# Weight conversion of a fused attention and two-MLP kernel: clamps moved to VectorE, rounding to ScalarE, cache writes to the sync queue, later loads spread, one more buffer set

## The chip, the cores and the metric

The kernel runs on one core of a Trainium2 chip. The metric is device microseconds of one execution, the median of several. A core has five engines that run side by side, each through its own list of instructions in a fixed order: TensorE (PE in the rows; PEld is its weight load), VectorE (DVE), ScalarE (ACT), GpSimd (POOL) and SyncE (SP, which here only issues DMAs). ACT issues some DMAs too (its rows are ACTq). An engine that waits for something holds up everything that stands behind it in its list.

## What is computed

The weights of both MLPs come as float64, everything else as float32. Shortened:

```python
def reference(q, k, v, phi, w_in, w_out, moe2...):
    a = softmax(phi, axis=sequence)                   # 4 batches x 8 heads, 576 tokens, 32 memories
    k_m, v_m = a^T @ k, a^T @ v                       # 32 x 64 each
    x = softmax(q @ k_m^T / 8) @ v_m                  # heads joined: 2304 x 512
    h = x @ w_in                                      # 512 -> 2048
    x = (h * sigmoid(1.702 * h)) @ w_out              # 2048 -> 512
    xn = x / sqrt(mean(x * x) + 1e-6) * rms_g
    g = xn @ w_gate                                   # 512 -> 1536
    return (g * sigmoid(g) * (xn @ w_val)) @ w_o2     # 1536 -> 512
```

## The kernel before

**Passes.** The four batches are two pairs (batches 0 and 1, batches 2 and 3). A batch has two units of four heads, so a pair has four units, named (batch, half). The first MLP goes over its hidden units in 8 groups of 256, once for each pair; `a_g1` makes a group's hidden values for a quarter of a pair's tokens, `a_g2` adds their product with `w_out` to the sum `x2`. The second MLP then goes over 6 groups (`b_g3`, `b_g4`) for all tokens. The RMS norm of a pair (`norm_1` to `norm_4`) lies between.

**Products.** Every float32 product is three passes on TensorE: a value is a high part (rounded to a shorter format) plus a low part (the rest). `copy` makes the high part and `sub_lo` the low part; both are helpers, so all their instructions have the lines L102 (copy on GpSimd), L106 (copy on another engine) and L109.

**Weights.** A group's weights are loaded as raw float64 halves of 128 x 512 (`w_load`, three raw buffers) and turned into float32 by bit operations (`w_conv`): absolute value on ACT (L152), clamp (L153), shift and mask (L157), sign (L161), low bits (L164) on DVE, then the high and low part. What the first pair's pass has worked out for the first MLP is written to a cache in device memory (L168), from which the second pair's pass loads it (L127). Of the 68 halves that are converted from float64, 32 belong to the first MLP and 36 to the second.

**Attention of a pair** runs ahead of its pass: `ld_phi` and `ld_src` load phi, k, v and q of a unit (144 KB twice, then 576 KB each), `att_k1` to `att_k5` make k_m and v_m, `att_q1` to `att_q4` the softmax. The second pair's four units are side work (`att_side`) that is issued between the first pair's groups, before time 300 us. A unit's k, v and q take one of six large buffers, which units, the transposed softmax and x2 share.

**Order.** The source issues steps by hand-written tables; a scheduler then sets the order of each engine's list, so an edit of one step can move others. PSUM and SBUF buffers come from pools that rotate. `gf`, the result of the gelu in `a_g1`, has three buffers of the tag "val", shared by both halves of a group.

**DMAs** take turns on eight semaphore lanes: a DMA on a lane waits in its engine's list until the DMA that had the lane before has landed, whichever engine issued it.

Of the kernel before, what the change touches and what calls it, by code (L numbers as in the profile page):

```python
# [18 lines left out]
def kernel(  # L19
# [14 lines left out]
    """Every float32 product is taken as three float32r passes: x = h + l exactly, h being x  # L34
    rounded to float32r, and x*y = h*h' + l*h' + h*l' in float32 accumulation.

    Attention: attn @ v_m @ w_in is taken as attn @ (v_m @ w_in), per batch and head. Two batches
    (a pair) share the array when v_m @ w_in is worked out. The MLPs run feature-major over blocks
    of their hidden units (256 wide), so each weight is loaded and split once per pass; the sums
    over blocks are kept in SBUF.  # L40

    Columns of a pair: batch, parity, chunk pair, p, for token 6 p + 2 (chunk pair) + parity.
    """
# [7 lines left out]
    P = 128  # L51
# [11 lines left out]
    MINW = 2.0**-15  # bits 0x38000000  # L63
    MAXW = 122872.0  # bits 0x47EFFC00
# [47 lines left out]
    # The first MLP's float32 weights, as they are worked out on the first pass over them.  # L112
# [29 lines left out]
    def w_conv(hf, clamp=G, to_h=G, to_l=G):  # L142
        """float64 to float32, on the bits: sign and top exponent bit, then the other exponent
        bits and the fraction 3 to the left. What is out of float32's range is clamped."""
# [3 lines left out]
        else:  # L148
# [4 lines left out]
            clamp.tensor_scalar(  # L153
# [13 lines left out]
            if hf[0] == "a":  # L167
                nc.scalar.dma_start(out=cached(hf), in_=t.bitcast(F32))  # L168
# [5 lines left out]
        copy(to_h, h[:, c], x)  # L174
        sub_lo(to_l, l[:, c], x, h[:, c])

# [1 line left out]
    # A unit is four heads of a batch. Where its k and v lay, q^T and the softmax of its scores follow.  # L178
    # The four 32-row blocks of an odd batch hold heads 2, 3, 0, 1.
# [245 lines left out]
        # An odd batch's heads 2, 3, 0, 1 lie in its blocks, so the rows' halves  # L425
        # are of different batches.
# [14 lines left out]
    gt, x2 = {}, {}  # L441

    def a_g1(pr, g, t):
# [4 lines left out]
        for fc in range(2):  # L448
# [10 lines left out]
            gf = tmp.tile([P, TB], F32, tag="val", name="gf")  # L459
# [194 lines left out]
    def do(step):  # L654
        step[0](*step[1:])
# [15 lines left out]
    # Side work of each pass, in the order of its issue.  # L671
    def att_side():
        for u in [(2, 0), (2, 1), (3, 0), (3, 1)]:
            yield ld_unit, u
# [6 lines left out]
            yield from att_q(u, G)  # L681
# [30 lines left out]
    # Batch 0 first: its share of the first MLP runs beside the rest of batch 1's attention.  # L712
    for s in (
# [11 lines left out]
        (att_k5, b0), (att_k5, b1), (w_load, w0[3]), (w_conv, w0[1], G, A), (vm_part, 0, 0, 0),  # L725
        (vm_part, 0, 0, 1), (att_q4, a0, 0), (att_q4, a1, 1), (att_q4, a0, 1), (w_conv, w0[2]),
        (att_q4, a1, 0), (narrow,), (att_q1, b1, 1), (w_conv, w0[3], G, A), (w_load, w1[0]),
        (att_q1, b0, 0), (w_load, w1[1]), (w_conv, w1[0], G, A), (att_q1, b1, 0), (att_q3, b1, 1),
# [88 lines left out]
```

## Time and profile before

| | |
|---|---|
| device time, median of 3 runs | 922.57 us (921.31 to 928.22) |
| the profiled execution: span from first to last instruction | 919.6 us |
| busy: PE, PEld, DVE, ACT, POOL | 866.3, 823.1, 556.7, 382.2, 496.5 us |
| instructions | 14798 |

The profiled execution is told by its span; its own time is not listed apart. The span leaves out what lies before the first and after the last instruction, and the median of the runs stands 3.0 us above it. Rows name an engine, a line of the source (L153), an operation and the tiles that it writes and reads; a time in square brackets or behind "idle before" is how long that engine had nothing to run, with what ended the wait.

### The profile page before, as it was taken

Reading aid. Unit: us, or ns where it says so; the run is one execution under the profiler, and the core shown is the slowest. Engines: PE = TensorE matmul, PEld = TensorE weight load, DVE = VectorE, ACT = ScalarE, POOL = GpSimd, SP = SyncE. Lnnn points to the kernel's source line nnn. Section 1 sums busy time; section 2 is a strip of 40 time slices with the busy share of each in tenths; the row PEclk is TensorE's granted clock in tenths of the full one; section 3 lists DMA queues with packets and bytes.
Section 4 is the critical chain, followed back from the end, with each engine's and each line's share of the span. In section 5 each row is a group of like instructions: output and inputs, shape, how many; then the busy total and the mean of one; then the engine's idle time right before and its main releaser. Section 6 shows DMA issues by size and latency. Waiting matters only on the chain.

```text
span 919.6 us, 14798 instructions
## 1 busy us (share of the span) xinstructions
PE 866.3 (94%) x5702; PEld 823.1 (90%) x5702; DVE 556.7 (61%) x997; ACT 382.2 (42%) x823; POOL 496.5 (54%) x450
## 2 busy tenths in 40 slices
PE   3887997997999999999998999999999999999997
PEld 2776997986999999999988999999999999999997
DVE  5699896788965456558778155366348328333333
ACT  2366773654667765554466342122122122111110
POOL 2377998897987695979994162064046018001000
PEclk9989998999999999999999999999999999999999
DMA  9974559433221120223313021012004001000123
GB/s 215 258 218 124 165 137 244 160 118 108 90 70 46 48 69 25 69 73 101 92 47 92 1 92 46 1 46 92 0 1 124 14 1 47 1 1 1 46 58 103
DMA packets 40534, 74.62 MB, mean 81 GB/s; under 512 B 3856, under 2 KB 16144, under 8 KB 40464
## 3 DMA queue, kind: packets, MB, share of 16 engines
q1 hardware_dynamic: 35856, 65.29, 26.2%
q10 hardware_dynamic: 4608, 8.39, 2.6%
q8 instruction: 45, 0.74, 0.3%
q14 instruction: 25, 0.20, 0.1%
HBM read 60.56 MB, written 13.11 MB: 80 GB/s over the span
## 4 chain that ended last, share of the span: by engine, by line
PE 72%; POOL 8%; DVE 7%; DMA 6%; issue 4%; SPq 2%; ACT 1%; ACTq 0%; POOLq 0%; DVEq 0%
PE pg L577 31%; PE pg L608 16%; PE pg L483 14%; PE pg L454 7%; POOL cv L153 2%; DMA stage<-in_k_dram 2%; DVE cv L161 2%; PE pvm L422 2%; DMA raw_a_out<-in_moe_w_out_dram 2%; POOL gr L109 2%; DVE cv L164 1%; DVE x L491 1%; DMA stage<-in_v_dram 1%; DVE cv L157 1%; DMA raw_a_in<-in_moe_w_in_dram 1%
## 5 line engine op out<-in xcount | busy, mean ns | idle before, releaser
L483 PE MATMUL pg<-gr,a_outh 128*128 128x288 f32 x1024 | 231.4, 301 | 11.7 <-DVE x L491 10.2
L483 PEld LDWEIGHTS pg<-gr,a_outh 128*128 128x128 f32 x1024 | 172.8, 190 | 16.4 <-DVE x L491 14.7
L483 PE MATMUL pg<-gr,a_outl 128*128 128x288 f32 x512 | 151.6, 297 | 0.0
L153 POOL TENSOR_SCALAR cv<-cv 128x512 f32<-128x512 f32 x67 | 137.1, 2051 | 22.8 <-ACT cv L152 20.8
L608 PE MATMUL pg<-b_o2h,pp 128*128 128x512 f32 x432 | 139.7, 391 | 0.0
L586 DVE TENSOR_TENSOR pf<-sg,pg 128x384 f32<-128x384 f32 x72 | 39.6, 552 | 158.2 <-PE pg L577 151.0
L109 POOL TENSOR_TENSOR gr<-gf,gr 128x288 fp32r<-128x288 f32 x128 | 115.9, 920 | 34.8 <-ACT gr L462 30.1
L491 DVE TENSOR_TENSOR x<-x,pg 128x288 f32<-128x288 f32 x224 | 95.9, 446 | 61.8 <-PE pg L483 60.7
L102 POOL TENSOR_SCALAR b_o2h<-cv 128x512 fp32r<-128x512 f32 x12 | 8.4, 716 | 223.6 <-PE pg L577 223.4
L584 ACT ACTIVATE sg<-pg 128x384 f32<-128x384 f32 x72 | 35.4, 492 | 159.1 <-PE pg L577 159.0
L483 PEld LDWEIGHTS pg<-gr,a_outl 128*128 128x128 f32 x512 | 97.1, 190 | 0.0
L608 PEld LDWEIGHTS pg<-b_o2h,pp 128*128 128x128 f32 x432 | 81.1, 188 | 16.1
L588 ACT CAST pp<-pf 128x384 fp32r<-128x384 f32 x72 | 37.0, 513 | 126.9 <-DVE pf L586 126.6
L608 PE MATMUL pg<-b_o2l,pp 128*128 128x512 f32 x216 | 84.8, 393 | 0.0
L616 DVE TENSOR_TENSOR oacc<-oacc,pg 128x512 f32<-128x512 f32 x90 | 61.1, 683 | 24.1 <-PE pg L608 24.1
L460 ACT ACTIVATE gf<-pg 128x288 f32<-128x288 f32 x128 | 51.6, 410 | 53.4 <-POOL gr L109 25.2
L109 DVE TENSOR_TENSOR pp<-pf,pp 128x384 fp32r<-128x384 f32 x72 | 46.3, 643 | 34.9 <-ACT pp L588 34.9
L462 ACT CAST gr<-gf 128x288 fp32r<-128x288 f32 x128 | 53.5, 432 | 28.8 <-PE pg L483 25.3
L577 PE MATMUL pg<-xnh,b_gateh 128*128 128x384 f32 x288 | 62.6, 337 | 0.0
L577 PE MATMUL pg<-xnh,b_vall 128*128 128x384 f32 x288 | 62.3, 337 | 0.0
L577 PE MATMUL pg<-xnh,b_gatel 128*128 128x384 f32 x288 | 62.3, 336 | 0.0
L157 DVE TENSOR_SCALAR cv<-cv 128x512 uint32<-128x512 uint32 x68 | 52.0, 765 | 17.0 <-POOL cv L153 16.9
(183 smaller groups left out, 1849.4 us busy)
## 6 DMA issues: line engine op xcount, KB each, us to landing
raw_a_in<-in_moe_w_in_dram SPq DMA_DIRECT2D x16, 512.0 KB, 4.2
raw_a_out<-in_moe_w_out_dram SPq DMA_DIRECT2D x16, 512.0 KB, 4.3
cache<-cv ACTq DMA_DIRECT2D x32, 256.0 KB, 3.8
raw_b_gate<-in_moe_w_gate_dram SPq DMA_DIRECT2D x12, 512.0 KB, 3.7
raw_b_val<-in_moe_w_val_dram SPq DMA_DIRECT2D x12, 512.0 KB, 3.8
raw_b_o<-in_moe_w_out_dram SPq DMA_DIRECT2D x12, 512.0 KB, 3.6
stage<-in_k_dram SPq DMA_DIRECT2D x8, 576.0 KB, 12.1
stage<-in_v_dram SPq DMA_DIRECT2D x8, 576.0 KB, 11.6
```

What stands on the lines that cost most here:

```text
L109: eng.tensor_tensor(out=lo, in0=full, in1=hi.bitcast(F32), op=ALU.subtract)
L153: clamp.tensor_scalar(out=t.bitcast(F32), in0=t.bitcast(F32), scalar1=MINW, scalar2=MAXW, op0=ALU.max, op1=ALU.min,)
L157: nc.vector.tensor_scalar(out=t, in0=t, scalar1=3, scalar2=0x3FFFFFFF, op0=ALU.logical_shift_left, op1=ALU.bitwise_and,)
L454: nc.tensor.matmul(ps[:, :HALF], lhsT=a[:, b, c, f], rhs=at[:, y, c, n], start=(i == 0), stop=(i == 5),)
L460: nc.scalar.activation(out=gf[:, :HALF], in_=ps[:, :HALF], func=AF.Gelu_apprx_sigmoid)
L462: nc.scalar.copy(out=gr[:, 0, :HALF], in_=gf[:, :HALF])
L483: nc.tensor.matmul(ps[:, :HALF], lhsT=wo[a][:, fc, es], rhs=gr[fc][:, y, :HALF], start=(i == 0), stop=(i == 5),)
L491: nc.vector.tensor_tensor(out=acc[:, e, n], in0=acc[:, e, n], in1=ps[:, :HALF], op=ALU.add)
L577: nc.tensor.matmul(ps[:, :TB], lhsT=w[a][:, e, f], rhs=xs[y][:, e, n], start=(i == 0), stop=(i == 3 * NE - 1),)
L586: nc.vector.tensor_tensor(out=pf, in0=sg, in1=pss[1][:, :TB], op=ALU.mult)
L608: nc.tensor.matmul(ps, lhsT=pp[fc][:, a, ks], rhs=w[y][:, fc], start=(i == 0), stop=(i == 5))
L616: nc.vector.tensor_tensor(out=o, in0=o, in1=ps, op=ALU.add)
```

## The change

It does five things. The clamp of every converted half runs on VectorE (before: 67 of 68 on GpSimd). The high part of a freshly converted half is rounded on ScalarE (before: 62 of 68 on GpSimd, 6 on ScalarE by hand); halves that come from the cache stay on GpSimd. Cache writes are issued by SyncE instead of ScalarE. The loads of the second pair's units 2 to 4 are issued one by one beside the query steps of the unit before, instead of at the head of their own unit. The gelu's second half takes a buffer of the tag "sg" (three buffers that only the second MLP used). In the start-up table the arguments that had put single steps elsewhere are dropped, and one half's low part goes to VectorE as before.

```diff
-    def w_conv(hf, clamp=G, to_h=G, to_l=G):
+    def w_conv(hf, to_h=None, to_l=G):
...
-            clamp.tensor_scalar(
+            nc.vector.tensor_scalar(
                 out=t.bitcast(F32), in0=t.bitcast(F32), scalar1=MINW, scalar2=MAXW,
...
             if hf[0] == "a":
-                nc.scalar.dma_start(out=cached(hf), in_=t.bitcast(F32))
+                nc.sync.dma_start(out=cached(hf), in_=t.bitcast(F32))
...
-        copy(to_h, h[:, c], x)
+        copy(to_h or (G if hf[:2] == ("a", 1) else A), h[:, c], x)
         sub_lo(to_l, l[:, c], x, h[:, c])
...
-            gf = tmp.tile([P, TB], F32, tag="val", name="gf")
+            gf = tmp.tile([P, TB], F32, tag=("val", "sg")[fc], name="gf")
...
     def att_side():
-        for u in [(2, 0), (2, 1), (3, 0), (3, 1)]:
-            yield ld_unit, u
+        us = [(2, 0), (2, 1), (3, 0), (3, 1)]
+        yield ld_unit, us[0]
+        for u, nxt in zip(us, us[1:] + [None]):
             yield att_k1, u
...
-            yield from att_q(u, G)
+            for i, step in enumerate(att_q(u, G)):
+                if nxt and i % 2 == 1:
+                    do(((ld_phi, nxt), (ld_src, nxt, 0), (ld_src, nxt, 1), (ld_src, nxt, 2))[i // 2])
+                yield step
...
-        (w_conv, w1[1], G, A), (w_conv, w2[0], V, A), (a_g2, 0, 0, 0), (aside,),
+        (w_conv, w1[1]), (w_conv, w2[0]), (a_g2, 0, 0, 0), (aside,),
...
-        (w_conv, w2[1], G, G, V), (a_g1, 0, 1, 1), (w_load, w2[3]), (a_g1, 0, 1, 2),
+        (w_conv, w2[1], A, V), (a_g1, 0, 1, 1), (w_load, w2[3]), (a_g1, 0, 1, 2),
```

The first place is VectorE near the start, where the first two weight halves (`cv_164`, `cv_499`) meet the first unit's scores (`stage0_0`):

```order
-L369 TENSOR_REDUCE stage0_0_119<-pq3_314 96x12
-L373 TENSOR_TENSOR stage0_0_119<-pq3_314,stage0_0_119 96x6x64
+L153 TENSOR_SCALAR cv_164<-cv_164 128x512
 L157 TENSOR_SCALAR cv_164<-cv_164 128x512
 L161 SCALAR_TENSOR_TENSOR cv_164<-raw_a_0_0_in_0_159,cv_164 128x512
+L369 TENSOR_REDUCE stage0_0_119<-pq3_314 96x12
+L153 TENSOR_SCALAR cv_499<-cv_499 128x512
+L164 SCALAR_TENSOR_TENSOR cv_164<-raw_a_0_0_in_0_159,cv_164 128x512
+L373 TENSOR_TENSOR stage0_0_119<-pq3_314,stage0_0_119 96x6x64
```

Two clamps came into the list, and the softmax steps of the first unit (L369, L373) now stand behind the conversion of the first half instead of ahead of it.

The second place is SyncE where the second pair's units are loaded (`stage2_1` is unit (2, 1)). Before, three units stand in one run, ahead of the weights of groups 4 and 5:

```order
L133 DMA raw_a_0_4_out_0_1804<-in_moe_w_out_dram 128x1024
L209 DMA stage2_1_1443<-in_k_dram 96x4x384
L209 DMA stage2_1_1443<-in_v_dram 96x4x384
L209 DMA stage2_1_1443<-in_q_dram 96x4x384
L209 DMA stage3_0_2169<-in_k_dram 96x4x384
L209 DMA stage3_0_2169<-in_v_dram 96x4x384
L209 DMA stage3_0_2169<-in_q_dram 96x4x384
L209 DMA stage3_1_2826<-in_k_dram 96x4x384
L209 DMA stage3_1_2826<-in_v_dram 96x4x384
L209 DMA stage3_1_2826<-in_q_dram 96x4x384
L133 DMA raw_a_0_4_out_1_1891<-in_moe_w_out_dram 128x1024
```

With the change, the same place:

```order
L168 DMA cache_102<-cv_1803 128x512
L133 DMA raw_a_0_4_out_1_1904<-in_moe_w_out_dram 128x1024
L198 DMA kmisc3_0_1816<-in_phi_dram 96x2x192 x2
L209 DMA stage3_0_1906<-in_k_dram 96x4x384
L209 DMA stage3_0_1906<-in_v_dram 96x4x384
L209 DMA stage3_0_1906<-in_q_dram 96x4x384
L209 DMA stage3_1_2565<-in_k_dram 96x4x384
L209 DMA stage3_1_2565<-in_v_dram 96x4x384
L209 DMA stage3_1_2565<-in_q_dram 96x4x384
L168 DMA cache_102<-cv_1895 128x512
L135 DMA raw_a_0_5_in_0_1989<-in_moe_w_in_dram 128x2x512
```

Unit (2, 1) has left the run (its k now stands behind the load of `kmisc2_0`, its v and q two weight halves later), six loads still follow each other, and each cache write stands ahead of a weight load.

The third place is GpSimd while the third group's weights are made ready (`gr` is a gelu's low part in `a_g1`):

```order
-L102 TENSOR_SCALAR a_0_2_inh_871<-cv_1138 128x512
-L153 TENSOR_SCALAR cv_1221<-cv_1221 128x512
 L109 TENSOR_TENSOR gr_985<-gf_983,gr_985 128x288
-L153 TENSOR_SCALAR cv_1274<-cv_1274 128x512
+L295 MEMSET kz_2282 128x64
+L296 MEMSET kz_2282 128x64
 L109 TENSOR_TENSOR gr_997<-gf_995,gr_997 128x288
 L109 TENSOR_TENSOR gr_1065<-gf_1063,gr_1065 128x288
-L153 TENSOR_SCALAR cv_1421<-cv_1421 128x512
```

Clamps and rounding left the list, so the low parts of the gelu follow each other.

## Rows read from the trace of the kernel before

**Rows 1.** Busy time of each engine (instructions), granted clock, DMA share, by stretch.

```profile
core 0: us, PE busy (x) PEld busy (x) DVE busy (x) ACT busy (x) POOL busy (x), PEclk, DMA share, GB/s
0.00:46.00 46.00, 27.97 (x272) 23.47 (x276) 26.02 (x59) 12.49 (x32) 15.38 (x25) 1.00 1.04 237
46.00:92.00 46.00, 36.35 (x295) 32.68 (x288) 42.73 (x81) 31.78 (x77) 34.24 (x29) 0.93 0.60 172
92.00:138.00 46.00, 43.60 (x339) 42.47 (x338) 39.62 (x76) 33.27 (x78) 44.02 (x41) 1.00 0.51 151
138.00:161.00 23.00, 17.32 (x112) 16.23 (x111) 13.99 (x26) 7.67 (x15) 18.70 (x16) 0.90 1.10 245
161.00:207.00 46.00, 43.78 (x366) 41.70 (x365) 38.62 (x78) 28.54 (x67) 41.76 (x37) 0.98 0.41 138
207.00:230.00 23.00, 17.23 (x153) 16.05 (x152) 18.94 (x26) 11.05 (x23) 18.11 (x16) 0.93 0.36 109
230.00:276.00 46.00, 45.50 (x399) 45.00 (x398) 37.94 (x79) 29.07 (x70) 41.03 (x40) 1.00 0.26 79
276.00:445.00 169.00, 168.83 (x1301) 168.28 (x1300) 102.54 (x211) 103.17 (x237) 138.07 (x143) 1.00 0.23 65
445.00:500.00 55.00, 50.82 (x299) 48.30 (x299) 45.67 (x71) 34.29 (x59) 44.56 (x33) 0.97 0.22 64
500.00:919.60 419.60, 414.92 (x2190) 388.98 (x2188) 190.66 (x298) 90.90 (x172) 100.59 (x75) 1.00 0.13 39
sum 919.60, PE 866.33 PEld 823.14 DVE 556.74 ACT 382.22 POOL 496.46; mean PE 86.63 PEld 82.31 DVE 55.67 ACT 38.22 POOL 49.65
```

**Rows 2.** Whom TensorE waited for, whole span: us in total, times, longest.

```profile
PE pk L229 <- DVE kmisc L222: 12.7, 4, 5.3
PE pg L483 <- DVE x L491: 10.2, 10, 5.2
PE pg L454 <- ACT gf L460: 4.0, 1, 4.0
PE pnr L535 <- DVE r L528: 3.4, 1, 3.4
```

**Rows 3.** ScalarE's list around 157 us: start, duration, idle before in brackets.

```profile
156.68 0.33 ACTq L168 DMA_DIRECT2D cache<-cv  x1
157.06 0.41 ACT L460 ACTIVATE gf<-pg 128x288 f32<-128x288 f32 x1 [7.65 <-DMA stage<-in_k_dram]
```

**Rows 4.** First and last of nine unit loads that SyncE issued in one run.

```profile
131.73 0.42 SPq L209 DMA_DIRECT2D stage<-in_k_dram  x1
...
141.51 3.73 SPq L209 DMA_DIRECT2D stage<-in_q_dram  x1
```

**Rows 5.** VectorE's list, three instructions beside GpSimd's.

```profile
82.36 0.83 DVE L153 TENSOR_SCALAR cv<-cv 128x512 f32<-128x512 f32 x1
83.22 0.43 DVE L157 TENSOR_SCALAR cv<-cv 128x512 uint32<-128x512 uint32 x1
...
213.88 5.53 DVE L161 SCALAR_TENSOR_TENSOR cv<-raw_a_out,cv 128x512 uint32<-128x512 uint32 x1
```

**Rows 6.** GpSimd's clamp beside the first two of those.

```profile
81.99 2.22 POOL L153 TENSOR_SCALAR cv<-cv 128x512 f32<-128x512 f32 x1
```

**Rows 7.** Clamps on GpSimd and shifts on VectorE in 46 to 276 us: busy, mean ns.

```profile
L153 POOL TENSOR_SCALAR cv<-cv 128x512 f32<-128x512 f32 x28 | 58.0, 2073 | 4.5 <-ACT cv L152 3.8
...
L157 DVE TENSOR_SCALAR cv<-cv 128x512 uint32<-128x512 uint32 x29 | 21.0, 723 | 2.7 <-POOL cv L153 2.6
```

**Rows 8.** VectorE's shift L157, all 68: duration in ns, min/median/max.

```profile
L157 DVE TENSOR_SCALAR cv<-cv x68: 357/794/1515, 34.1 to 780.3; 128x512 uint32<-128x512 uint32 x68
```

**Rows 9.** Rounding that ScalarE already did for the first MLP's w_in.

```profile
L106 ACT CAST a_inh<-cv 128x512 fp32r<-128x512 f32 x4 | 2.5, 622 | 2.3 <-DVE attnT L109 2.3
```

**Rows 10.** ScalarE's issues of cache writes: ns min/median/max, first and last start.

```profile
L168 ACTq DMA_DIRECT2D cache<-cv x32: 326/342/379, 37.2 to 252.4; - x32
```

**Rows 11.** ScalarE's gelu waiting for GpSimd's low part: us, times, longest.

```profile
ACT gf L460 <- POOL gr L109: 25.2, 25, 4.7
```

More of the change, by code (lines that the diff above doesn't have):

```diff
@@ L724 @@
         (att_q3, a1, 0), (att_q3, a1, 1), (att_q3s, a1, 1, G), (att_k4, b1), (att_q3s, a1, 0, G),
-        (att_k5, b0), (att_k5, b1), (w_load, w0[3]), (w_conv, w0[1], G, A), (vm_part, 0, 0, 0),
+        (att_k5, b0), (att_k5, b1), (w_load, w0[3]), (w_conv, w0[1]), (vm_part, 0, 0, 0),
         (vm_part, 0, 0, 1), (att_q4, a0, 0), (att_q4, a1, 1), (att_q4, a0, 1), (w_conv, w0[2]),
-        (att_q4, a1, 0), (narrow,), (att_q1, b1, 1), (w_conv, w0[3], G, A), (w_load, w1[0]),
-        (att_q1, b0, 0), (w_load, w1[1]), (w_conv, w1[0], G, A), (att_q1, b1, 0), (att_q3, b1, 1),
+        (att_q4, a1, 0), (narrow,), (att_q1, b1, 1), (w_conv, w0[3]), (w_load, w1[0]),
+        (att_q1, b0, 0), (w_load, w1[1]), (w_conv, w1[0]), (att_q1, b1, 0), (att_q3, b1, 1),
         (att_q3, b1, 0), (aside,), (att_q1, b0, 1, V), (att_q3s, b1, 1, V), (aside,),
@@ L731 @@
         (att_q3, b0, 0), (aside,), (w_load, w1[3]), (att_q4, b1, 0), (att_q3s, b0, 1, G),
-        (att_q3s, b0, 0, V), (att_q4, b0, 0), (att_q4, b0, 1), (w_conv, w1[2], G, A),
+        (att_q3s, b0, 0, V), (att_q4, b0, 0), (att_q4, b0, 1), (w_conv, w1[2]),
         (att_q4, b1, 1), (w_load, w2[0]), (a_g1, 0, 0, 1), (a_g1, 0, 0, 2), (a_g2, 0, 0, 1),
-        (w_conv, w1[1], G, A), (w_conv, w2[0], V, A), (a_g2, 0, 0, 0), (aside,),
+        (w_conv, w1[1]), (w_conv, w2[0]), (a_g2, 0, 0, 0), (aside,),
         (vm_next, 0, 1, 0), (aside,), (vm_next, 0, 1, 1), (w_load, w2[1]), (a_g1, 0, 0, 3),
```

## Prediction

> **What bounds the kernel now.** I read the stretches first [rows 1]: where TensorE is busy the whole stretch nothing can be won, so the table says where to look. From 276 to 445 us TensorE idles 0.2 of 169 us and from 500 to the end 4.7 of 419.6, which is the drain behind the last matmul. Those 589 us stay, whatever the other engines do. The idle time lies in 0 to 46 (18.0 us), in 46 to 276 (9.7, 2.4, 5.7, 2.2, 5.8 and 0.5, together 26.2) and in 445 to 500 (4.2). The clock column adds a little: 0.90 from 138 to 161, 0.93 from 207 to 230, behind long idle times, where the stretches at 1.00 are almost without them.
>
> Second, who ends TensorE's waits [rows 2]. The largest group is the start, where L229 waits for the first maxima of phi while the input arrives; the DMA engines are full there (share 1.04 and 237 GB/s [rows 1]). Then come three single waits: 4.0 us for the gelu, 5.2 us for VectorE's add into x2 (its group has ten waits, 10.2 us), 3.4 us in the norm. The rest are many short ones.
>
> Third, which engine is full where TensorE idles. From 46 to 276 us POOL is busy 197.9 of 230 us and DVE 191.8, but not alike: from 92 to 138 it is POOL (44.0 of 46), and from 46 to 92 it is DVE (42.7 of 46, POOL 34.2), and there TensorE idles most. ACT has room, 141.4 of 230. So the change takes work from one nearly full engine and gives some to another nearly full one; that is the question of this case.
>
> **GpSimd's clamps go.** In 46 to 276 us they are 28 instructions of 2.07 us, 58.0 us [rows 7]. POOL then has at most 140 us of work in 230, less the roundings that leave too. It stops being a bound there. ACT's gelu waits for POOL 25 times, 25.2 us [rows 11]; few of these reach TensorE, since ACT has slack.
>
> **VectorE's clamps come.** The trace has one such clamp: 0.83 us [rows 5]. The nearest row with many is the shift L157, which has the same size and kind (one input, two constants, SBUF to SBUF): 0.357 us at least, 1.515 at most [rows 8], 0.723 on average in this stretch [rows 7]. So 28 clamps cost 10 to 42 us of DVE time. I take between 0.43, a shift that ran while POOL clamped [rows 5, 6], and the mean 0.723: 12.0 to 20.2 us.
>
> What does DVE get back? L161 at 213.88 lasted 5.53 us [rows 5], where a shift of the same size takes 0.723, and it lies in the stretch (207 to 230) in which TensorE idles 5.8 us. No row names what held it; I take it to be POOL's work, which is two-input there, and count on a pause now that 58 us of it are gone: 5.53 - 0.72 = 4.8 us back. That POOL's clamps themselves hold DVE up, the rows don't say: while POOL clamped from 81.99 to 84.21, a shift on DVE took 0.43 us, close to its least [rows 5, 6, 8].
>
> The Trainium skill (SBUF — State Buffer, section "Who interferes with whom") has GpSimd and VectorE share a port pair that one instruction holds for its whole length, while the other fully blocks. By it that shift should have waited until the clamp ended at 84.21; the trace does not agree for this clamp, and it would agree for the 5.53 us step. What the rule would give if it held for most clamps stands below as a rival.
>
> DVE's work from 46 to 276 becomes 191.8 + 12.0 - 4.8 = 199.0 us, or 191.8 + 20.2 - 4.8 = 207.2. Where DVE sets the pace now, it reaches 42.7 of 46, 93%. At that share the stretch takes 199.0/0.93 = 214 us or 207.2/0.93 = 223 us instead of 230: 16 or 7 us less. Counted from TensorE, the two long waits are 4.0 + 5.2 = 9.2 us, and the clock behind them gives 17.3 x 0.10 + 17.2 x 0.07 = 2.9: 12.1 us. The two ways meet at **-10 us**, which I take; most of the short waits stay, or new ones take their place, since DVE is fuller than before.
>
> **Rounding on ScalarE** costs 0.62 us each [rows 9]. Some 25 more in this stretch are 16 us, on an engine with 89 us of room; the cover is that room, and if it failed, a rounding would hold up the gelu behind it by 0.6 us at a time. I cost it at nothing. Where ACT waits for DVE's last step (L164) to round, the gelu waits as well; that is new for most halves and belongs to the share of short waits that I leave standing.
>
> **Cache writes and unit loads.** The 4.0 us wait has its cause in [rows 3]: ScalarE stood still 7.65 us at the issue of a cache write, until a unit's k had landed, and the gelu behind it in the list came late. Nine unit loads were issued from 131.73 to 141.51 [rows 4], 5.3 MB at 245 GB/s [rows 1]. With cache writes on SP no gelu stands behind a DMA any more, and the loads of one unit go out in the stretches before, where the DMA share is 0.60 and 0.51 against 1.10 [rows 1]. Six loads stay in a run (second place in the order), but only SP waits for them. The issues themselves, 32 of 0.34 us [rows 10], leave an engine with slack: nothing. On SP each cache write now stands ahead of a weight load. That load already needed the same last step of DVE, because it reuses the raw buffer which that step reads; so it comes later by one issue, 0.34 us, beside buffers that hold three halves. I cost it at nothing; 32 x 0.34 = 11 us is the most if every one were on the path.
>
> The Trainium skill (DMA: Bandwidth & Descriptors, section "Issuing engines are not separate DMA queues") says that issuing from several engines saves only issue time, since all use the same DMA engines. By that alone this edit would win nothing here; the trace differs, since the 7.65 us were a wait at the issue and not bandwidth.
>
> **The gelu's second half** in buffers of its own frees the gelu from POOL's low part two steps back. The 25 waits are ACT's [rows 11]; TensorE waited once for the gelu, for the other cause. Nothing, at most 1 us.
>
> **The start** (0 to 46). DVE's list now runs the first half's clamp, shift and sign ahead of the first unit's softmax (first place in the order). Against that stand two or three clamps of 2.07 us that become some 0.7 us, so 3 to 4 us less from landing to a converted half. The stretch is held by arrivals. I take 0 and keep 3 us on either side.
>
> **The norm** (445 to 500). POOL is busy 44.6 of 55 us, with clamps between the sums of squares, and TensorE waits 3.4 us for their end [rows 1, 2]. Without the clamps the sums come earlier; the wait goes: **-3.4 us**. DVE is busy 45.7 of 55 here, so the wait can return on DVE: bounds 0 and -5.7 (all 4.2 idle and 0.03 x 50.8 of clock).
>
> **Sum.** -10 - 3.4 = -13.4. The profiled span is 919.6, which would become 906.2; the median is 3.0 above the span, so 922.6 - 13.4 = 909.2: **909 us**.
>
> **Rivals.**
> VectorE takes the bound over and eats the gain. With 0.723 to 1.0 us for a clamp and no gain in the norm, 46 to 276 takes 207.2/0.93 = 223 to (191.8 + 28.0 - 4.8)/0.93 = 231 us: -7 to +1, so 915 to 924. For it: 42.7 of 46 us with TensorE idle. Against it: DVE idles 9 us from 138 to 161, which conversions can fill once weights come sooner.
>
> VectorE gets slower, and the kernel with it. POOL's list now has low parts back to back, each reading SBUF (third place in the order). If DVE's one-input steps find no pause, a clamp costs 1.515 and nothing comes back: (191.8 + 42.4)/0.93 = 252 us, +22, less 3.4 in the norm: 941. It decides from the clamp's price: more than 1% slower needs 242.6 x 0.93 = 225.6 us of DVE work, so 1.21 us per clamp. The median shift, 0.794 [rows 8], speaks against it.
>
> POOL's clamps did block DVE, as the port rule has it. Then 29 shifts fall from 0.723 to 0.357, 10.6 us, and DVE has 199.0 - 10.6 = 188.4 us of work, 203 at 93%. TensorE's own 203.8 us of work set the end then, with a few short waits some 208: -22, and -5 in the norm: 895.
>
> The spreading does little: six loads still in a run, weights of group 5 late behind them on the lanes, and TensorE's 4.0 us and its clock (1.7) come back as a wait for weights. -13.4 + 5.7 = -7.7: 915.
>
> **How the numbers follow.** Forecast (902 to 913) 0.44, DVE eats the gain 0.24, spreading does little 0.08, port relief 0.16, slower 0.08. About 1% (9.2 us) is what a measurement of this kernel can tell from no change. Faster by more than that holds the forecast and the port relief, 0.60; the same 0.32; slower 0.08. The range of 8 in 10 reaches down to the port relief, 896, and up through the DVE case, 924; it leaves out the slower case and the ends of the others.
>
> **What would show it.** In the changed profile: no ACT wait of several us at an issue or at a unit's landing near 157; POOL below 65% from 46 to 276; clamps on DVE of 0.43 to 0.75 us; DVE at 90% or more of that stretch, and TensorE's waits there mostly for DVE lines; no step of DVE above 3 us; the wait at L535 below 1 us; 276 to 445 and the end as before. I am wrong if DVE's clamps average over 1 us, if the start grows by more than 3 us, or if SP's weight loads behind cache writes become what a conversion waits for.

## The result, and the profile after

The changed kernel takes 927.4 us, the median of 19 runs (923.2 to 934.2), where the kernel before took 921.7 beside it. The ratio is 1.0061, with a 95% interval of 1.0045 to 1.0076: 0.6% slower, where 909 us were forecast. The profiled span grew from 919.6 to 924.1 us. Two executions that took far longer than all others, one of e9 below (2146.6 us) and one of the kernel before beside it (4726.9), count in the medians and in no percentage.

The stretches of the changed kernel, as in [rows 1]:

```profile
0.00:46.00 46.00, 29.60 (x286) 24.64 (x286) 28.10 (x66) 12.38 (x30) 11.21 (x22) 1.00 1.04 246
46.00:92.00 46.00, 29.80 (x198) 26.94 (x199) 38.28 (x83) 29.94 (x73) 18.99 (x19) 0.88 0.79 222
92.00:138.00 46.00, 44.02 (x370) 42.73 (x370) 37.45 (x76) 38.13 (x87) 24.20 (x25) 0.97 0.39 127
138.00:161.00 23.00, 18.93 (x131) 18.16 (x130) 22.76 (x34) 12.34 (x25) 13.85 (x12) 0.93 0.96 213
161.00:207.00 46.00, 44.59 (x385) 43.43 (x384) 41.96 (x88) 31.07 (x73) 24.80 (x26) 1.00 0.37 124
207.00:230.00 23.00, 20.21 (x185) 18.82 (x186) 19.25 (x43) 17.09 (x39) 10.02 (x10) 1.00 0.42 138
230.00:276.00 46.00, 46.00 (x406) 45.63 (x404) 31.89 (x71) 28.56 (x66) 33.05 (x36) 1.00 0.23 66
276.00:445.00 169.00, 165.16 (x1254) 163.54 (x1254) 110.19 (x215) 103.00 (x237) 122.54 (x130) 1.00 0.23 69
445.00:500.00 55.00, 48.68 (x288) 47.27 (x288) 34.32 (x66) 30.84 (x54) 22.09 (x19) 0.91 0.12 39
500.00:924.10 424.10, 419.42 (x2213) 393.13 (x2211) 192.80 (x330) 105.47 (x203) 41.15 (x26) 1.00 0.13 39
sum 924.10, PE 866.44 PEld 824.28 DVE 556.99 ACT 408.83 POOL 321.89; mean PE 86.64 PEld 82.43 DVE 55.70 ACT 40.88 POOL 32.19
```

Subtract TensorE's busy time from each length and set it beside [rows 1]. TensorE's sum of busy time is the same (866.4 and 866.3), so the difference of idle time is the result. Idle time falls by 1.6 us in 0 to 46 and by 6.3 in 92 to 276 (0.4, 1.6, 0.8, 3.0, 0.5). It rises by 6.5 in 46 to 92, by 3.7 in 276 to 445 and by 2.1 in 445 to 500. That makes +4.4 of the 4.5 us. The relief that was forecast is there, and more is lost at three other places. Each stretch is read from one profile. The start differs most from profile to profile: in the 20 profiles of this document TensorE idles 15.3 to 22.3 us in 0 to 46, so the 1.6 us there are not shown to come from the change.

Whom TensorE waited for, over the whole span, answers to [rows 2]:

```profile
PE pk L229 <- DVE kmisc L222: 12.1, 3, 5.4
PE pq L397 <- DVE stage L385: 9.7, 1, 9.7
PE pg L577 <- ACT sg L584: 4.9, 1, 4.9
PE pg L454 <- ACT gf L460: 3.9, 5, 1.3
PE pk L314 <- ACT kz L297: 3.0, 3, 2.2
PE pg L483 <- DVE x L491: 2.6, 5, 1.5
```

The three waits named before have shrunk (the gelu's longest from 4.0 to 1.3, x from 5.2 to 1.5; the norm's at L535 is gone from 445 to 500). Two single waits are new and larger: 9.7 us for a softmax and 4.9 us for the second MLP's sigmoid.

**The 9.7 us** end at 87.63 us. VectorE's list ahead of them (start, duration, instruction):

```profile
76.20 0.54 DVE L369 TENSOR_REDUCE stage<-pq 96x12 f32<-96x384 f32 x1
...
77.38 0.38 DVE L153 TENSOR_SCALAR cv<-cv 128x512 f32<-128x512 f32 x1
77.79 0.94 DVE L157 TENSOR_SCALAR cv<-cv 128x512 uint32<-128x512 uint32 x1
78.65 2.03 DVE L153 TENSOR_SCALAR cv<-cv 128x512 f32<-128x512 f32 x1
80.60 0.68 DVE L161 SCALAR_TENSOR_TENSOR cv<-raw_a_in,cv 128x512 uint32<-128x512 uint32 x1
81.21 0.54 DVE L378 TENSOR_REDUCE stage<-stage 96x12 f32<-96x384 f32 x1
...
83.30 0.16 DVE L381 TENSOR_SCALAR stage<-stage 96x12 f32<-96x12 f32 x1
83.38 0.68 DVE L161 SCALAR_TENSOR_TENSOR cv<-raw_a_out,cv 128x512 uint32<-128x512 uint32 x1
83.98 1.43 DVE L251 TENSOR_REDUCE kmisc<-kmisc 96x128 f32<-96x768 f32 x1
85.33 0.41 DVE L157 TENSOR_SCALAR cv<-cv 128x512 uint32<-128x512 uint32 x1
85.67 0.21 DVE L384 RECIPROCAL stage<-stage 96x12 f32<-96x12 f32 x1
85.80 0.62 DVE L164 SCALAR_TENSOR_TENSOR cv<-raw_a_out,cv 128x512 uint32<-128x512 uint32 x1
86.35 0.67 DVE L161 SCALAR_TENSOR_TENSOR cv<-raw_a_in,cv 128x512 uint32<-128x512 uint32 x1
86.94 0.54 DVE L385 TENSOR_TENSOR stage<-stage 96x384 f32<-96x384 f32 x1
```

The softmax of batch 1's last unit is four short steps (L378, L381, L384, L385; 0.54, 0.16, 0.21, 0.54 us). They are spread over 81.21 to 87.48, since conversion steps (L153, L157, L161, L164), which take 7.9 us together, stand in front of and between them. From that unit's last maximum (L369) to its last product, VectorE's list has 11 conversion steps. All 11 are of the next two groups' weights, which TensorE does not yet need. In the list before it was 1, and TensorE waited 2.7 us there:

```profile
75.11 0.48 DVE L369 TENSOR_REDUCE stage<-pq 96x12 f32<-96x384 f32 x1
...
75.59 0.68 DVE L164 SCALAR_TENSOR_TENSOR cv<-raw_a_in,cv 128x512 uint32<-128x512 uint32 x1
...
81.12 1.32 DVE L385 TENSOR_TENSOR stage<-stage 96x384 f32<-96x384 f32 x1
```

**The 4.9 us** have the same form. The norm's factors (rb) were ready at 478.37 us, 477.89 + 0.48 on ScalarE. VectorE's list goes on:

```profile
478.32 0.42 DVE L153 TENSOR_SCALAR cv<-cv 128x512 f32<-128x512 f32 x1
478.65 0.69 DVE L164 SCALAR_TENSOR_TENSOR cv<-raw_b_val,cv 128x512 uint32<-128x512 uint32 x1
479.26 1.24 DVE L157 TENSOR_SCALAR cv<-cv 128x512 uint32<-128x512 uint32 x1
480.53 0.69 DVE L161 SCALAR_TENSOR_TENSOR cv<-raw_b_o,cv 128x512 uint32<-128x512 uint32 x1
481.25 0.69 DVE L164 SCALAR_TENSOR_TENSOR cv<-raw_b_o,cv 128x512 uint32<-128x512 uint32 x1
481.86 1.67 DVE L549 SCALAR_TENSOR_TENSOR xnf<-x,rg,rb 128x384 f32<-128x384 f32 x3
```

So xnf (the normalized x) came 3.5 us late. ScalarE rounds xnf, takes a square for the next norm (L504) and copies output sums (L614) ahead of the sigmoid in its list, so the sigmoid is late too:

```profile
482.51 1.04 ACT L553 CAST xnh<-xnf 128x384 fp32r<-128x384 f32 x2 [3.72 <-DVE xnf L549]
...
486.03 0.51 ACT L584 ACTIVATE sg<-pg 128x384 f32<-128x384 f32 x1
```

What VectorE's conversions cost in 46 to 276 us, by line (busy, mean ns of one), beside [rows 7]:

```profile
L153 DVE TENSOR_SCALAR cv<-cv 128x512 f32<-128x512 f32 x29 | 19.9, 687 | 5.1 <-ACT cv L152 5.0
L157 DVE TENSOR_SCALAR cv<-cv 128x512 uint32<-128x512 uint32 x29 | 15.1, 521 | 0.2
```

### The profile page after: what moved, and what is told of

The parts are those of the page before. It is cut to its first block, busy times and chain, and to the rows that moved or that the text cites. A ratio compares the mean times of both kernels' runs of the same rounds, so it can differ in the third digit from the quotient of the medians.

```text
span 924.1 us, 14740 instructions
## 1 busy us (share of the span) xinstructions
PE 866.4 (94%) x5702; PEld 824.3 (89%) x5702; DVE 557.0 (60%) x1064; ACT 408.8 (44%) x883; POOL 321.9 (35%) x321
## 4 chain that ended last, share of the span: by engine, by line
PE 77%; DVE 8%; DMA 7%; ACT 5%; issue 2%; SPq 1%; POOL 1%; ACTq 0%; DVEq 0%
PE pg L577 32%; PE pg L483 16%; PE pg L608 16%; PE pg L454 8%; DMA raw_a_in<-in_moe_w_in_dram 3%; PE pvm L422 2%; DVE cv L164 1%; DVE cv L153 1%; DMA raw_a_out<-in_moe_w_out_dram 1%; DVE cv L161 1%; DMA stage<-in_v_dram 1%; DMA kmisc<-in_phi_dram 1%; DMA raw_b_gate<-in_moe_w_gate_dram 1%; PE pq L360 1%; DVE cv L157 1%
## 5 line engine op out<-in xcount | busy, mean ns | idle before, releaser
L483 PE MATMUL pg<-gr,a_outh 128*128 128x288 f32 x1024 | 234.3, 298 | 3.9 <-DVE x L491 2.6
L109 POOL TENSOR_TENSOR gr<-gf,gr 128x288 fp32r<-128x288 f32 x128 | 113.0, 897 | 118.9 <-ACT gr L462 116.9
L109 POOL TENSOR_TENSOR b_o2l<-cv,b_o2h 128x512 fp32r<-128x512 f32 x12 | 15.7, 1332 | 250.2 <-PE pg L577 159.8
L577 PE MATMUL pg<-xnh,b_valh 128*128 128x384 f32 x288 | 62.9, 338 | 4.9 <-ACT sg L584 4.9
L577 PE MATMUL pg<-xnl,b_gateh 128*128 128x384 f32 x288 | 62.8, 337 | 0.0
L577 PE MATMUL pg<-xnl,b_valh 128*128 128x384 f32 x288 | 62.4, 336 | 0.0
```

Source lines behind the costliest of these rows:

```text
L109: eng.tensor_tensor(out=lo, in0=full, in1=hi.bitcast(F32), op=ALU.subtract)
L483: nc.tensor.matmul(ps[:, :HALF], lhsT=wo[a][:, fc, es], rhs=gr[fc][:, y, :HALF], start=(i == 0), stop=(i == 5),)
L577: nc.tensor.matmul(ps[:, :TB], lhsT=w[a][:, e, f], rhs=xs[y][:, e, n], start=(i == 0), stop=(i == 3 * NE - 1),)
```

## The experiments

**Theories.** (1) The place in the list: a clamp on VectorE is cheap, but conversions no longer wait for GpSimd's 2 us, so the scheduler finds them ready earlier and puts them ahead of the short steps of softmax and norm. (2) The spread loads collide with the first pass's weights. (3) Rounding on ScalarE waits for VectorE's last step and holds up gelu and sigmoid. (4), added later: the gelu's second buffers cost something. Every percentage is against the kernel before on the same chip, with its 95% interval. Some kernels (e1, e7, e9, e11, e14) were profiled in an execution 4 to 9 us from their median, so stretches of one profile are used with care. "Steps" are conversion steps in VectorE's list from the last maximum (L369) to the last product (L385) of the last softmax of batch 1; the expectations of e1, e2, e3 and e5 counted them from the first maximum and give more.

**e1**, the clamps alone.

```diff
-            clamp.tensor_scalar(
+            nc.vector.tensor_scalar(
```

> The kernel before with one edit: all clamps on VectorE. Theory 1, the place in VectorE's list: a clamp is cheap (0.43 us by its median in the changed kernel), but with it the scheduler puts conversions earlier in VectorE's list, 7 and 9 conversion steps inside the last two softmaxes of batch 1 (before 1 and 6; in the changed kernel 8 and 11) and 5 and 3 steps ahead of the xnf of the second and third norm (before none). TensorE's idle time from 46 to 92 us grows from 9.7 to 13 to 17 us, in 445 to 500 from 4.2 to 6 to 8; some 4 us come back in 92 to 276: 922 to 928, the larger part of the changed kernel's loss. Theory 2, the earlier loads collide with the first pass's weights: the clamps are innocent, 46 to 92 stays at 9 to 10 us idle and GpSimd's relief shows: 912 to 918. Theory 3, ScalarE's rounding waits for VectorE and holds up gelu and sigmoid: also 912 to 918 here.

924.9 us, +0.23% [0.03, 0.44], in theory 1's range; theories 2 and 3 expected 912 to 918. TensorE waits 6.5 us for the last softmax, with 6 steps.

**e2**, the changed kernel with all clamps on GpSimd.

```diff
-            nc.vector.tensor_scalar(
+            G.tensor_scalar(
```

> The changed kernel with the clamps back on GpSimd, the four other edits kept. VectorE's list then has 0 and 6 conversion steps inside the two softmaxes, as before the change, and at most 1 step ahead of an xnf. Theory 1, the place in VectorE's list: 46 to 92 us falls from 16.2 to 9 to 11 us idle, 445 to 500 to about 4, and the gains of the cache writes and the spread loads stay (the 4.0 us gelu wait near 157 gone): 914 to 919. Theory 2, the loads collide: 46 to 92 keeps 14 us or more idle, 922 to 928. Theory 3, ScalarE's rounding: the 4.9 us wait for the sigmoid in 445 to 500 stays, 919 to 924.

923.1 us, +0.08% [-0.10, 0.25]. The softmax wait falls to 1.2 us, the idle time of 46 to 92 to 9.3; 445 to 500 idles 3.6, and the sigmoid's wait there falls from 4.9 to 1.1 although ScalarE still rounds, against theory 3. So beside the other four edits the clamps carry 0.5%, but those four do not gain what theory 1 expected of them.

**e3**, the rounding alone.

```diff
-    def w_conv(hf, clamp=G, to_h=G, to_l=G):
+    def w_conv(hf, clamp=G, to_h=None, to_l=G):
...
-        copy(to_h, h[:, c], x)
+        copy(to_h or (G if hf[:2] == ("a", 1) else A), h[:, c], x)
...
-        (w_conv, w2[1], G, G, V), ...
+        (w_conv, w2[1], G, A, V), ...
```

> The kernel before with one edit: the high part of a freshly converted half rounded on ScalarE. Theories 1 and 2: nothing that TensorE sees, 920 to 924; VectorE's list has 1 and 8 conversion steps in the two softmaxes (before 1 and 6), so at most 1 to 2 us more in 46 to 92. Theory 3, the roundings wait in ScalarE's list for VectorE's last step and hold up the gelu and the sigmoid behind them: 924 to 928, with TensorE waits for ScalarE of 3 us or more in 445 to 500.

930.6 us, +0.88% [0.62, 1.15]: theory 3's side, and 2.6 us above its range. One wait of 5.4 us for the gelu and one of 3.1 for the sigmoid.

**e4**, the cache writes alone.

```diff
-                nc.scalar.dma_start(out=cached(hf), in_=t.bitcast(F32))
+                nc.sync.dma_start(out=cached(hf), in_=t.bitcast(F32))
```

> The kernel before with one edit: cache writes issued by SyncE. All theories: ScalarE no longer stands at an issue near 157 us, the 4.0 us wait of TensorE for the gelu goes, and nothing else moves (0 and 6 conversion steps in the softmaxes): 917 to 921. If weight loads behind a cache write on SyncE come too late, new waits for a converted weight appear between 92 and 276 us and the time is 922 or more.

920.5 us, -0.23% [-0.46, 0.00]: as expected, small. No ScalarE wait at an issue, and TensorE's longest wait for the gelu is 1.7 us.

**e5**, the changed kernel with the rounding back on GpSimd.

```diff
-        copy(to_h or (G if hf[:2] == ("a", 1) else A), h[:, c], x)
+        copy(to_h or G, h[:, c], x)
```

> The changed kernel with the rounding of fresh halves back on GpSimd (only the two that the start-up table names stay off it); the clamps stay on VectorE. Theory 1, the place in VectorE's list, alone: 8 and 10 conversion steps still stand in the two softmaxes and 3, 1 and 2 ahead of the three xnf, so 46 to 92 us keeps 13 us or more of idle time: 924 to 928. Theory 3, ScalarE's rounding (alone it made the kernel before 0.9% slower): 8 us go, 917 to 921. If each edit only shuffles the lists and none has a price of its own, anything from 919 to 929 without the rows named here.

929.5 us, +0.67% [0.44, 0.89], 1.5 us above theory 1's range. Nothing comes back, so theory 3 does not carry the full change's loss. The softmax wait is 8.8 us, with 9 steps. One freshly converted half, not two, is still rounded on ScalarE.

**e6**, cache writes, spread loads and gelu buffers, without clamps and rounding: e4's edit, e7's and

```diff
-            gf = tmp.tile([P, TB], F32, tag="val", name="gf")
+            gf = tmp.tile([P, TB], F32, tag=("val", "sg")[fc], name="gf")
```

> The kernel before with cache writes on SyncE, the spread loads and the gelu's second half in buffers of its own; clamps and roundings as before. Theories 1 and 3 put the whole loss on the clamps and the roundings: this keeps the gains of the others, 914 to 919, with 46 to 92 us at 9 to 11 us idle and no wait of 4 us near 157. Theory 2, the loads collide with the first pass's weights: 922 to 927, with 46 to 92 at 13 us idle or more.

921.9 us, -0.20% [-0.42, 0.02], between the two expectations. 46 to 92 idles 7.9 us, so theory 2's collision in that stretch is not there.

**e7**, the spread loads alone.

```diff
...
-            yield from att_q(u, G)
+            for i, step in enumerate(att_q(u, G)):
+                if nxt and i % 2 == 1:
+                    do(((ld_phi, nxt), (ld_src, nxt, 0), (ld_src, nxt, 1), (ld_src, nxt, 2))[i // 2])
+                yield step
```

> The kernel before with one edit: the loads of the second pair's units 2 to 4 one by one beside the query steps. Theories 1 and 3: 919 to 923; ScalarE still stands at cache issues, so the gelu wait near 157 stays or moves. Theory 2: 46 to 92 us idle 13 us or more, 924 to 928.

926.8 us, +0.37% [0.11, 0.62], the time of theory 2 and not of theories 1 and 3; 46 to 92 idles 10.0 us, against theory 2. Its profile, 917.8 us, is of an execution much faster than its median, and doesn't tell where the loss lies.

**e8**, the changed kernel with the softmax's sums at a higher scheduler priority.

```diff
+        with tc.high_priority(100):
+            q3s(u, hp, eng)
```

> The changed kernel with the softmax sums and their product (att_q3s) at a higher priority for the scheduler: VectorE's list then has 7 conversion steps in the last softmax of batch 1 instead of 11, and one of its two products 19 rows earlier. Theory 1: TensorE's 9.7 us wait at 87 us shrinks to 5 us or less, 46 to 92 us idles 10 to 12 us, 921 to 924. Theory 2: the wait stays at 8 us or more, since the data are late. Theory 3: the wait in 46 to 92 may go, the loss in 445 to 500 stays, 924 to 927.

935.4 us, +1.22% [0.96, 1.49]. The 7 steps in the expectation were a miscount of mine: the list still has 11 there, and the wait is 10.0 us. So this repeats the changed kernel's place and says nothing for or against theory 1. It does say that an edit of the order alone, which leaves that place as it was, can cost 0.6%.

**e9**, three clamps back on GpSimd, those of the conversions inside the last softmax.

```diff
-        (w_conv, w1[1]), (w_conv, w2[0]), ...
+        (w_conv, w1[1]), (w_conv, w2[0], None, G, G), ...
```

(w1[3] and w2[1] alike; `w_conv` takes the engine as its last argument. The clamp of w2[0] ran on VectorE in the kernel before, too.)

> The changed kernel with three of its 67 moved clamps back on GpSimd: those of the halves whose conversion stood in the last softmax of batch 1 (third half-pair of group 1, first two of group 2). VectorE's list then has 1 conversion step between the last maximum and the last product of that softmax, not 11; ahead of the second pair's first xnf there are still 8. Theory 1, the place in the list: TensorE's wait for that product falls from 9.7 to 1 to 3 us, as in every kernel with 1 to 3 steps there, and the time by 6 to 8 us: 919 to 922. If VectorE's work as such, or the loads, were late, the wait stays above 7 us and the time at 925 to 928. If the wait goes and the same time is lost further on, 924 to 928 with the wait at 1 to 3 us.

930.1 us, +0.88% [0.56, 1.20]. The list has 1 step there and the wait fell from 9.7 to 3.9 us, but the time did not fall. This is nearest to the third case of the expectation, gained there and lost further on: 46 to 92 idles 12.2 us for 16.2, 92 to 276 idles 17.0 for 10.2, in a profile 6 us above the median.

**e10**, two more back, those of the halves ahead of xnf.

```diff
-        (norm_1, 1, 1), (w_conv, h1[0]), ... (w_conv, h0[5]), ...
+        (norm_1, 1, 1), (w_conv, h1[0], None, G, G), ... (w_conv, h0[5], None, G, G), ...
```

> As the run before, with two more clamps back on GpSimd: those of the two halves whose 8 conversion steps stood between the norm's reciprocal and its first xnf; none stands there then. Theory 1: besides the 9.7 us wait, the 4.9 us wait for the sigmoid behind the late xnf goes or falls below 3 us, 445 to 500 us idles about 4 and not 6.3: 914 to 918. If the sigmoid's wait comes from ScalarE's rounding (theory 3) or from gelu buffers taken from the sigmoid, it stays and the time is that of the run before.

928.1 us, +0.64% [0.45, 0.83], where theory 1 expected 914 to 918. Whom TensorE waited for in 440 to 505 us:

```profile
PE pnr L535 <- DVE r L528: 4.8, 1, 4.8
```

The sigmoid's wait is gone, and a wait for the norm's reciprocal as long as it stands in its place. The mechanism of both waits is confirmed: the steps go, and the waits go with them. That they are the price of the change is not: without them the time is the same.

**e11**, the gelu's buffers alone, by the two lines of e6.

> The kernel before with one edit: the gelu's second half in buffers of the sigmoid's tag. Theory 4, drawn from the end of the first MLP: the kernels with this edit reach the last hidden step 3 to 7 us earlier and have lost it again by 500 us, since gelu halves run ahead of the sums and hold buffers that the sigmoid needs; alone it makes 922 to 927, with TensorE waits of 3 us or more for the sigmoid. Theories 1 and 3: no price, GpSimd's hold on the gelu falls from 25 waits to about 12, 917 to 922.

928.8 us, +0.60% [0.36, 0.84]: theory 4's side, 1.8 us above its range; the longest wait for the sigmoid is 2.9 us. In 276 to 445 us, where the kernel before has no wait, TensorE waits:

```profile
PE pg L454 <- ACT gf L460: 2.5, 2, 2.1
PE pg L483 <- DVE x L491: 2.2, 2, 1.9
```

Over the whole span, however, TensorE idles 53.5 us there, and 53.3 in the kernel before. In this profile, 11.3 us longer than that one, the loss lies in TensorE's busy time (877.4 and 866.3 us for the same matmuls) and not in its waits, so how the buffers cost time is open.

**e12**, cache writes and spread loads together, the edits of e4 and e7.

> The kernel before with cache writes on SyncE and the spread loads, and nothing else. If the gelu's buffers cost what theory 4 says (these two with it came to 0.2% under the kernel before), 914 to 918; if they cost nothing, 919 to 923. TensorE's wait for the last softmax of batch 1 is 1 to 3 us in both cases, since 1 conversion step stands in it.

921.7 us, -0.28% [-0.48, -0.08]. Nearer the second expectation: beside these two the gelu's buffers (e6) cost 0.1%, not 0.6%. Edits that alone cost +0.37% and -0.23% together gain.

**e13**, e12 and all clamps, the line of e1.

> Cache writes on SyncE, spread loads and all clamps on VectorE; roundings and gelu buffers as before. The same without the clamps stood 0.3% under the kernel before. Theory 1, the clamps are the price in the company of the others, by VectorE's list (again 8 and 11 conversion steps in the last two softmaxes of batch 1): TensorE waits 8 to 10 us there and the time is 924 to 928. Theory 4, the gelu's buffers are the price: 918 to 922.

927.8 us, +0.60% [0.45, 0.75], as theory 1 expected: the clamps cost 0.9% in this company. The softmax wait is 10.4 us with 11 steps.

**e14**, e12 and the rounding, the lines of e3.

> Cache writes on SyncE, spread loads and fresh halves rounded on ScalarE; clamps and gelu buffers as before. Theory 3, ScalarE's rounding has a price of its own (alone it cost 0.9%): 926 to 930. If that price came only from how it shuffled the lists, most of it is gone where the lists differ: 919 to 923.

931.7 us, +1.19% [0.88, 1.49]: theory 3's side, 1.7 us above its range. But with clamps or gelu buffers beside it the same rounding costs 0.3% or gains (table below). Its profile, 9 us above the median, shows a cause that no theory named: VectorE stands at the first maximum of a later unit's phi until the spread load has landed, and the sum x, for which TensorE waits, stands behind it in the list:

```profile
165.33 1.44 DVE L222 TENSOR_REDUCE kmisc<-kmisc 96x128 f32<-96x768 f32 x1 [7.30 <-DMA kmisc<-in_phi_dram]
...
167.79 0.61 PE L483 MATMUL pg<-gr,a_outh 128*128 128x288 f32 x1 [8.47 <-DVE x L491]
```

The longest such wait of VectorE from 46 to 276 is 6.1 us in e2, 5.6 in e6, 1.8 in the changed kernel and 0.8 before.

**e15**, the changed kernel without the gelu buffers, e6's two lines undone.

> The changed kernel with the gelu's second half back in the buffers of the first. Theory 4: the waits that the kernels with split buffers show near 340 us (1.3 to 2.1 us for the gelu) and near 425 to 444 us (1 to 2 us for vm or x) are gone, 276 to 445 us idles under 1 us as before, and the time is 4 to 5 us less than the changed kernel's: 921 to 924. Theory 1: the wait at 87 us stays at 8 to 10 us, and the clamps hold the time at 924 to 928.

920.8 us, -0.13% [-0.30, 0.04]. Theory 4's side, and more than it expected: 276 to 445 idles 1.8 us, not 3.8, and 0.7% comes back although the softmax wait is still 10.0 us and the sigmoid's 4.9. So a kernel with both waits in it need not be slower than the kernel before. Of the 6.0 us between the two profiles, 5.3 are busy time of TensorE (866.4 and 861.1).

**e16**, e12 and, on VectorE, only the clamps of groups 3 to 7 (20 of 67), besides the one that ran there before.

```diff
-            clamp.tensor_scalar(
+            (V if hf[0] == "a" and hf[2] > 2 else clamp).tensor_scalar(
```

> Cache writes on SyncE, spread loads, and on VectorE only the 20 clamps of groups 3 to 7 of the first MLP, which are converted after the first pair's attention and before the norm; all others on GpSimd. Theory 1, a clamp on VectorE costs where short steps of softmax or norm stand behind conversions: 1 step in the last softmax, none ahead of an xnf, so no price, and GpSimd's relief from 100 to 276 us shows: 914 to 918. If clamps on VectorE cost wherever they stand, or the list only moves its waits: 921 to 926.

915.2 us, -0.66% [-0.91, -0.41], as theory 1 expected. The softmax wait is 1.6 us.

**e17**, the changed kernel with only those 20 clamps on VectorE.

```diff
-            nc.vector.tensor_scalar(
+            (V if hf[0] == "a" and hf[2] > 2 else G).tensor_scalar(
```

> The changed kernel, but on VectorE only the 20 clamps of groups 3 to 7 of the first MLP; those ahead of them and those of the second MLP back on GpSimd. Theory 1, the place decides the clamps' price: 1 conversion step stands in the last softmax of batch 1 and at most 1 ahead of an xnf, TensorE waits 1 to 3 us at that softmax, 46 to 92 us idles 9 to 11, and the 20 clamps give the 3 to 4 us that they gave beside cache and spread: 917 to 921. Theories 3 and 4, rounding and gelu buffers carry a price of their own: 923 to 927, with the waits near 340 and 425 us.

917.2 us, -0.76% [-1.07, -0.44], as theory 1 expected, with rounding and gelu buffers in place. Its rows of the stretches that had lost, in 46 to 92 and from 276:

```profile
46.00:92.00 46.00, 35.15 (x260) 31.75 (x264) 39.09 (x85) 29.93 (x75) 34.93 (x28) 0.78 0.78 204
...
276.00:445.00 169.00, 165.69 (x1255) 164.14 (x1254) 107.24 (x203) 100.30 (x234) 133.46 (x135) 1.00 0.21 62
445.00:500.00 55.00, 51.66 (x316) 49.42 (x316) 42.58 (x73) 34.95 (x63) 37.77 (x26) 1.00 0.22 64
```

TensorE idles 10.9 us in the first (the changed kernel 16.2), at a clock of 0.78 and not 0.88, and 3.3 in the last (6.3), at the full clock and not 0.91. The 3.3 us in 276 to 445 stay, as with the gelu's buffers elsewhere.

**e18**, the 20 clamps alone, e16's line on the kernel before.

> The kernel before with one edit: the 20 clamps of groups 3 to 7 on VectorE. Up to that place the lists are those of the kernel before. Theory 1: the clamps gain where nothing short stands behind them, 138 to 276 us idles 7 to 10 us and not 14, 916 to 920. If the gain of the run with cache and spread came from its other lists: 921 to 924.

920.9 us, -0.14% [-0.36, 0.08]: just above the first expectation. 138 to 276 idles 10.9 us, not 14.2, where 7 to 10 were expected. By themselves the 20 clamps show no gain that is clear of noise; beside the others they gain 0.4 to 0.8%.

## Why the prediction was wrong

**What held.** A clamp costs what was said: 29 of 0.687 us in 46 to 276. GpSimd's busy share there is 54% (124.9 us), no ScalarE wait lies at an issue near 157, x's wait is 1.5 us, and the gelu waits for GpSimd 13 times, 10.7 us, where [rows 11] have 25 times and 25.2, both over the whole span (in 46 to 276: 4 times and 3.8 us, before 9 and 9.3). The start stayed inside its 3 us. VectorE got more back than the 4.8 us of the one long step: its other conversion steps (L157, L161, L164) fell from 81.3 to 65.3 us, so 19.1 us of added clamps cost 3.1 net, and all of VectorE's work stayed (191.8 and 191.6 us). The Trainium skill (SBUF — State Buffer, section "Who interferes with whom") has GpSimd and VectorE hold one port pair against each other, where VectorE's step reads two inputs from SBUF or runs in a two-port mode. In sum the trace agrees (16.0 us back), though the clamp of [rows 6] held up nothing. So the port relief of the third rival came too, and the 895 us that it was to give did not. Two signs failed: VectorE is busy for 83% of that stretch and not 90%, and one clamp took 4.16 us where no step was to be above 3. The reading that the stretches at a clock of 1.00 are almost without idle time leaves out 0 to 46, with 18.0 us.

**The step that failed** is the one in "VectorE's clamps come" that turns VectorE's work into time at 93% and into -10 us. Work on VectorE was no bound: it was to become 199 to 207 us, it stayed at 191.6, and 46 to 276 still took 0.2 us more idle time, not 10 less. The two long waits that the second way counted did go. What set the largest new wait was which step stood ahead of which. In all 20 kernels the wait at the last softmax of batch 1 goes with the conversion steps from its last maximum to its last product:

| conversion steps there | kernels | TensorE's wait, us |
|---|---|---|
| 1 to 3 | before, e2 to e4, e6, e7, e9 to e12, e14, e16 to e18 | 0.7 to 3.9 |
| 6 | e1 | 6.5 |
| 9 | e5 | 8.8 |
| 11 | changed kernel, e8, e13, e15 | 9.7 to 10.4 |

The rival of VectorE taking over the gain had its place (VectorE) and nearly its time (915 to 924), for another reason: the longest new waits go with the order of its list, and its load did not grow. "The norm, -3.4" failed in the same way: the wait left L535 and came back behind a late xnf as 4.9 us, 2.1 us more idle time, and 445 to 500 fell to a clock of 0.91 from 0.97. The prediction had named that return as a bound and had capped it at 0. "276 to 445 as before" failed by 3.7 us, which goes with the gelu's buffers, costed at nothing: of the nine kernels that have them, eight idle 3.3 to 4.9 us there (e2 1.3), of the eleven without, ten idle 0.2 to 2.1 (e13 3.9). The unit loads, of which the prediction said that only SP waits for them, held VectorE up to 7.3 us (e14).

**How far the causes are shown.** The cause of the two new waits is shown: they come and go with the conversion steps (table above, e9, e10). That they are the 0.6% is not shown: e9 shortens the first, e10 that and the second, and neither is faster; e15 keeps both and is not slower than the kernel before. That the choice of clamps decides what they are worth is shown by e16 and e17 against e13 and the changed kernel: the same edit on 20 halves gains where on 67 it loses, 1.3 to 1.4% apart. Whether that is their place, as theory 1 has it, or their number is not separated, since no run moves 20 others; nor is it known which of the other 47 carry the loss.

Two more things go with the times, and no run separates them. TensorE's busy time for the same 5702 matmuls runs from 861.1 us (e15) to 877.4 (e11) in the profiles, and of the 7.7 us between the changed kernel and e17, 4.4 are busy time and 3.3 idle time. And the mean granted clock of all executions is 0.979 for the changed kernel, 0.982 to 0.985 for the kernel before beside the experiments, 0.991 for e16 and 0.992 for e17. Whether shorter waits raised the clock, or the clock made a part of the gain by itself, is open.

That rounding or gelu buffers have a fixed price is refuted by the eight combinations on top of cache writes and spread loads:

| percent against before | without gelu buffers | with |
|---|---|---|
| no clamps, no rounding | -0.28 (e12) | -0.20 (e6) |
| clamps | +0.60 (e13) | +0.67 (e5) |
| rounding | +1.19 (e14) | +0.08 (e2) |
| clamps and rounding | -0.13 (e15) | +0.61 (changed kernel) |

Rounding ranges from -0.7 to +1.5, gelu buffers from -1.1 to +0.7. The cells are not quite alike: e2, e5, e15 and the changed kernel have the new start-up table and the others the old one, so that "no rounding" leaves one half on ScalarE in e5 and six in e12, e13 and e6. Every edit makes the scheduler write new lists for all engines, and e8 shows that a shift of the order alone can be worth 0.6%. Why e14 is so slow and e15 is not was settled only as far as the late phi in e14's profile.

**The best version** is e17 or e16 (917.2 and 915.2 us; their intervals overlap): 0.7% under the kernel before.

## What to carry to other kernels

Before an operation moves to another engine, count in that engine's new list what now stands ahead of the short steps that the bounding engine waits for; busy shares don't tell it. Such a count tells where the engine will wait, not what the whole kernel will take. A step that becomes ready sooner can be queued sooner than it is wanted, so move the work first where nothing short stands behind it (e16 and e17 did, and were the only versions more than 0.5% faster). Where a scheduler rewrites all lists at each edit, single edits don't add up, and under 1% only the combination that is to be kept can be judged.

## What was not expected of the hardware

VectorE's steps became shorter once the clamps left GpSimd: the shift L157 has a median of 419 ns over all 68 where it had 794 [rows 8], and 420 in e1, which moves the clamps alone:

```profile
L157 DVE TENSOR_SCALAR cv<-cv x68: 361/419/1407, 31.1 to 781.6; 128x512 uint32<-128x512 uint32 x68
L153 DVE TENSOR_SCALAR cv<-cv x68: 377/424/4156, 30.6 to 780.8; 128x512 f32<-128x512 f32 x68
```

Yet GpSimd's clamps are not what held the shift most often. Over the 20 traces, a shift that started while a GpSimd clamp ran had ended before that clamp in 101 of 123 cases; while a low part (L109, two inputs) ran, in 38 of 292; while a rounding (L102) ran, in 3 of 82. In the kernel before the shift starts behind GpSimd's clamp [rows 7] and so beside GpSimd's next step; that it took longer for that reason is not shown. The clamp at 78.65 took 2.03 us while a two-input step of GpSimd ran from 78.41 to 80.40:

```profile
78.41 1.99 POOL L244 TENSOR_TENSOR kmisc<-kmisc 96x768 f32<-96x768 f32 x1
```

Where GpSimd's steps followed each other without a pause, single short VectorE steps lasted several us here, and TensorE waited behind them. One clamp of the changed kernel took 4.16 us (from 138.49), and TensorE then waited 2.4 us for a `vm` part. In e12 a shift took 7.23 us beside seven such steps:

```profile
147.29 7.23 DVE L157 TENSOR_SCALAR cv<-cv 128x512 uint32<-128x512 uint32 x1
...
156.14 0.61 PE L483 MATMUL pg<-gr,a_outh 128*128 128x288 f32 x1 [5.83 <-DVE x L491]
```

The 5.53 us step of [rows 5] is of this kind, too: it began at 213.88 beside GpSimd steps that left no pause from 213.54 to 218.87, and TensorE's 5.2 us wait for x ended behind it.

TensorE's clock made a long wait dearer. Around the 9.7 us the granted clock went to 0.50, the lower level of 1.2 GHz, and stayed there for TensorE's first work after it:

```profile
84.00:88.00 4.00, 0.37 (x3) 0.40 (x4) 4.00 (x8) 0.62 (x1) 0.85 (x1) 0.50 0.76 254
88.00:92.00 4.00, 3.72 (x19) 3.43 (x18) 1.00 (x4) 1.90 (x4) 1.22 (x1) 0.50 0.93 312
```
